# Spectral filter and token-shift MLP, two layers each: all queues in a written order, zero frequency left out, norm scale put into the first table

## The chip, the cores and the metric

The kernel runs on one core of a Trainium2 chip. The time is the device time in microseconds. The engines named here are TensorE (PE, with its weight loads as PEld), VectorE (DVE), ScalarE (ACT), GpSimd (POOL) and SyncE (SP, which here only issues DMAs). Each engine works through its own queue in order. Matmul results go to PSUM, which is used as eight banks of 128 x 512 float32.

## The reference

A row state x of 2048 x 512 goes through two pairs of layers: a spectral filter (A) and a token-shift MLP (B). Both take a normalized x and add their result to x.

```
def _A_ref(x, w_r, w_i):
    X = rfft2(x.astype(float32), axes=(-2, -1))
    X = X * (w_r + 1j * w_i)                      # w: 2048 x 257
    return irfft2(X, s=(S, D)).astype(bfloat16)

def _B_ref(x, w1, w2, w3, w4):
    h = gelu(layernorm(x) @ w1)                   # 512 -> 512
    # four column quarters of h, shifted by +1, -1, +2, -2 rows
    x1 = x + concatenate([g0, g1, g2, g3]) @ w2   # 512 -> 512
    return x1 + gelu(layernorm(x1) @ w3) @ w4     # 512 -> 1792 -> 512

x = x + A(layernorm(x)); x = x + B(layernorm(x))
x = x + A(layernorm(x)); x = x + B(layernorm(x))
```

## The kernel before

The 2048 rows are split as p x q: 128 on partitions, 16 tiles q of 128 x 512. The state x stays in SBUF as bfloat16 (`x_state`). The transform over the 2048 rows is done in two factors, 128 and 16; the transform over the 512 columns is one matrix with 256 real and 256 imaginary columns.

`load_all` issues the DMAs (x, the tables, the filter weights W, the MLP weights). `first_stats` computes the sums of the first norm. `fix_weights` prepares the two purely real frequencies, column 0 and column 256, which share a place: it reads W on POOL (`cw`, L263 and L264), mirrors it by a small matmul (`ps_cw`, L266 and L268) and writes a corrected first column and a factor `beta`.

`layer_A` has four loops one after the other. For each q, DVE subtracts the mean and scales (`xn`, L224), PE multiplies by the 128-point table T (`ps_V`, L295) and the result is copied to V. For each of 16 blocks b, PE transforms the columns (`ps_TV`, L310), ACT copies (`TV`, L313), PE makes the 16-point step (`ps_X`, L315 to L317), ACT copies (`X`), and after every second block DVE multiplies by W (`Pa`, `Pb`, `Z`). After every fourth block a mirrored column 0 is added (`ps_mir`, then five POOL steps). Then, for each b, PE does the inverse 16-point step (`ps_M`, L352 and L353), copied to M. Then, for each q, PE does the inverse over columns (`ps_Y`, L370), ACT copies (`Y`, L373), PE does the inverse 128-point step (`ps_y`, L375) and DVE adds to x with a sum (L376); ACT computes the sum of squares (L196), and per group of four q's POOL computes the norm (`finish`, ten small steps).

`layer_B` works on four groups of four q's: `w1(g)` normalizes (L224), transposes on PE (`pt`, L388) with a copy on ACT (`xT`, L391), multiplies (`ps_h`, L416) and applies GELU on ACT (`hT`, L418); ACT also writes the normalized row `xb` (L411). `w2(g)` multiplies the shifted rows (`ps_x`, L432), DVE adds `xb` (L433), the norm and transposes follow. `w3` (`ps_g`, L451) and `w4` (`ps_o`, L462) are 224 matmuls each a layer.

The program is written loop after loop, and a scheduler of the framework puts the instructions of each engine in order; the pools (eight PSUM banks in one ring, `stream` with four buffers) set what may be in flight. The diff touches almost the whole program.

## Time and profile before

| | before |
|---|---|
| time, median of 3 runs (lowest to highest) | 607.88 us (604.0 to 610.07) |
| profiled execution: time, span | 607.9 us, 606.1 us |
| PE busy | 419.0 us (69%), 2022 matmuls |
| ACT busy | 282.1 us (47%) |
| DVE busy | 172.4 us (28%) |
| POOL busy | 85.4 us (14%) |
| mean granted TensorE clock | 0.900 |

The profile is one execution. Busy matmul time counts the pipelined duration of each matmul, so the spacing of matmuls in a dense stretch tells more than the mean duration. A row of the groups gives the line, the engine, output and inputs by name, the shapes, the count, then busy time, mean ns of one, and the idle time of that engine before these instructions with what ended it. A row of the waits reads "engine, what it would run, what it waited for: total us, times, longest".

### The profile page before, as it was taken

Reading aid. Unit: us, or ns where it says so; the run is one execution under the profiler, and the core shown is the slowest. Engines: PE = TensorE matmul, PEld = TensorE weight load, DVE = VectorE, ACT = ScalarE, POOL = GpSimd, SP = SyncE. Lnnn points to the kernel's source line nnn. Section 1 sums busy time; section 2 is a strip of 40 time slices with the busy share of each in tenths; the row PEclk is TensorE's granted clock in tenths of the full one; section 3 lists DMA queues with packets and bytes.
Section 4 is the critical chain, followed back from the end, with each engine's and each line's share of the span. In section 5 each row is a group of like instructions: output and inputs, shape, how many; then the busy total and the mean of one; then the engine's idle time right before and its main releaser. Section 6 shows DMA issues by size and latency. Waiting matters only on the chain.

```text
span 606.1 us, 5633 instructions
## 1 busy us (share of the span) xinstructions
PE 419.0 (69%) x2022; PEld 202.2 (33%) x2060; DVE 172.4 (28%) x441; ACT 282.1 (47%) x530; POOL 85.4 (14%) x248
## 2 busy tenths in 40 slices
PE   0046675544666697999996667365567566999997
PEld 0033243112233343444443325111224333444443
DVE  5253453222044321111026446312122333010111
ACT  6124554556655565353424545455654555614310
POOL 5410110232111101011011010222200111000000
PEclk9999999676888797999998999957976889899999
DMA  9993000000000000000000000000000000010001
GB/s 299 106 335 136 1 1 0 0 0 2 0 1 1 0 1 0 1 1 1 0 1 1 1 1 1 1 0 0 1 0 1 1 1 1 0 36 10 26 27 43
DMA packets 12267, 15.70 MB, mean 26 GB/s; under 512 B 1104, under 2 KB 10192, under 8 KB 11984
## 3 DMA queue, kind: packets, MB, share of 16 engines
q1 hardware_dynamic: 11952, 14.79, 9.8%
q10 hardware_dynamic: 288, 0.56, 0.2%
q8 instruction: 16, 0.26, 0.2%
q14 instruction: 11, 0.09, 0.0%
HBM read 13.25 MB, written 2.10 MB: 25 GB/s over the span
## 4 chain that ended last, share of the span: by engine, by line
PE 57%; ACT 16%; DVE 9%; POOL 7%; issue 5%; DMA 5%; SPq 0%; POOLq 0%; ACTq 0%; DVEq 0%
PE ps_g L451 17%; PE ps_o L462 16%; PE ps_TV L310 5%; PE ps_h L416 5%; ACT junk L196 3%; POOL ln_r L216 3%; DVE xb L433 3%; ACT TV L313 3%; ACT xT L391 3%; DMA W<-in_A_w_i_dram 3%; PE ps_Y L370 3%; ACT Y L373 2%; PE ps_y L375 2%; PE pt L388 2%; ACT xb L411 2%
## 5 line engine op out<-in xcount | busy, mean ns | idle before, releaser
L451 PE MATMUL ps_g<-xT,w 128*128 128x512 bf16 x436 | 103.8, 394 | 1.0 <-issue 0.4
L462 PE MATMUL ps_o<-w,gT 128*128 128x512 bf16 x440 | 97.2, 379 | 0.4
L453 ACT ACTIVATE gT<-ps_g 128x512 bf16<-128x512 f32 x112 | 66.6, 597 | 54.9 <-PE ps_g L451 41.9
L196 ACT ACTIVATE junk<-x_state 128x512 bf16<-128x512 bf16 x64 | 40.0, 625 | 65.6 <-DVE x_state L468 37.2
L451 PEld LDWEIGHTS <-w 128*128 128x128 bf16 x448 | 45.4, 102 | 55.2 <-issue 6.7
L462 PEld LDWEIGHTS <-gT 128*128 128x128 bf16 x448 | 43.9, 98 | 52.8
L388 PE MATMUL pt<-ident,xn 128*128 128x128 bf16 x256 | 26.7, 286 | 37.1 <-DVE xn L224 37.1
L208 POOL TENSOR_SCALAR ln_m<-ln_s 128x4 f32<-128x4 f32 x24 | 7.3, 303 | 307.2 <-DVE xb L433 131.4
L375 PE MATMUL ps_y<-Y,Tinv 128*128 128x512 bf16 x32 | 15.4, 480 | 50.5 <-ACT Y L373 50.5
L416 PE MATMUL ps_h<-xT,w 128*128 128x512 bf16 x122 | 36.1, 452 | 20.1 <-ACT xT L391 19.6
L433 DVE SCALAR_TENSOR_TENSOR xb<-ps_x,xb 128x512 bf16<-128x512 f32 x32 | 21.6, 687 | 98.5 <-PE ps_x L432 98.3
L391 ACT ACTIVATE xT<-pt 128x1024 bf16<-128x1024 bf16 x32 | 31.2, 1027 | 34.2 <-PE pt L388 34.2
L370 PE MATMUL ps_Y<-G,M 128*128 128x512 bf16 x124 | 43.7, 479 | 2.2 <-DVE M L357 0.9
L376 DVE SCALAR_TENSOR_TENSOR x_state<-ps_y,x_state 128x512 bf16<-128x512 f32 x32 | 22.1, 691 | 73.1 <-PE ps_y L375 73.1
L370 PEld LDWEIGHTS <-M 128*128 128x128 bf16 x128 | 14.5, 114 | 79.6 <-issue 71.5
L388 PEld LDWEIGHTS <-xn 128*128 128x128 bf16 x256 | 23.5, 132 | 45.8 <-DVE xn L224 41.1
L310 PE MATMUL ps_TV<-FA,V 128*128 128x512 bf16 x122 | 35.6, 404 | 2.4 <-DVE V L301 1.8
L411 ACT ACTIVATE xb<-x_state,ln_nmr,ln_r 128x512 bf16<-128x512 bf16 x32 | 24.4, 804 | 26.0 <-POOL ln_nmr L220 26.0
L465 DVE TENSOR_TENSOR x_state<-ps_o,x_state 128x512 bf16<-128x512 f32 x16 | 11.1, 692 | 76.8 <-PE ps_o L462 76.8
L468 DVE SCALAR_TENSOR_TENSOR x_state<-ps_o,x_state 128x512 bf16<-128x512 f32 x16 | 11.1, 691 | 72.2 <-PE ps_o L462 72.2
L216 POOL TENSOR_TENSOR ln_r<-ln_ve,mhalf 128x4 f32<-128x4 f32 (+1 forms) x24 | 30.3, 1261 | 2.0
L318 ACT ACTIVATE X<-ps_X 128x512 bf16<-128x512 f32 x32 | 19.1, 597 | 22.9 <-PE ps_X L317 22.9
(84 smaller groups left out, 468.4 us busy)
## 6 DMA issues: line engine op xcount, KB each, us to landing
w<-in_B_w_dram SPq DMA_DIRECT2D x2, 1792.0 KB, 15.2
x_state<-in_A_x_dram SPq DMA_DIRECT2D x8, 256.0 KB, 5.4
out_dram<-x_state SPq DMA_DIRECT2D x16, 128.0 KB, 1.8
TL<-tab_TL SPq DMA_DIRECT2D x1, 1536.0 KB, 8.5
TR<-tab_TR SPq DMA_DIRECT2D x1, 1536.0 KB, 10.7
w<-in_B_w_dram SPq DMA_DIRECT2D x2, 512.0 KB, 10.7
W<-in_A_w_r_dram SPq DMA_DIRECT2D x7, 128.5 KB, 9.6
W<-in_A_w_i_dram SPq DMA_DIRECT2D x7, 128.5 KB, 8.7
```

Of the source, the lines that this page charges most:

```text
L196: K.nc.scalar.activation(junk[:], src, ACT.Square, bias=0.0, scale=1.0, accum_out=self.ss[:, i:i + 1])
L216: e.tensor_tensor(self.r[:, 0:n], ve[:, 0:n], K.mhalf[:, 0:n], op=ALU.pow)
L310: nc.tensor.matmul(ps[:], lhsT=V[:, t, b].rearrange("d q c -> d (q c)"), rhs=K.FA[:, t, :], start=(t == 0), stop=(t == 3))
L370: nc.tensor.matmul(ps[:], lhsT=M[:, F, e, q, :], rhs=K.G[:, F, e, :], start=(n == 0), stop=(n == 3))
L388: nc.tensor.transpose(pt[:, (i % 2) * 4 + t, :], src[:, t * P:(t + 1) * P], K.ident[:])
L391: nc.scalar.activation(xT[:, :, o:o + 2 * P].rearrange("p t (h c) -> p t h c", h=2), pt[:].rearrange("p (h t) c -> p t h c", h=2), ACT.Cop ...
L411: nc.scalar.activation(xb[:, q, :], K.x[:, q, :], ACT.Identity, bias=L.nmr[:, i:i + 1], scale=L.r[:, i:i + 1])
L416: nc.tensor.matmul(ps[:], lhsT=K.w1[:, t, j * P:(j + 1) * P], rhs=xT[:, t, :], start=(t == 0), stop=(t == 3))
L433: nc.vector.scalar_tensor_tensor(xb[:, q, :], ps[:], 1.0, xb[:, q, :], op0=ALU.mult, op1=ALU.add, accum_out=L.s[:, i:i + 1])
L451: nc.tensor.matmul(ps[:], lhsT=K.w3[:, c, t * P:(t + 1) * P], rhs=xT[:, c, :], start=(c == 0), stop=(c == 3))
L453: nc.scalar.activation(gT[:, t, :], ps[:], ACT.Gelu_apprx_tanh, bias=0.0, scale=1.0)
L462: nc.tensor.matmul(ps[:], lhsT=gT[:, t, i * P:(i + 1) * P], rhs=K.w4[:, t, :], start=(t == 0), stop=(t == 13))
```

## The change

The framework's scheduler is switched off: each engine's queue is the order in which the program is written, and the program is written anew for that.

- *Zero frequency.* A normalized row has mean zero, so frequency 0 of the columns is zero. The table now holds frequencies 1 to 256, and frequency 256 alone takes the last imaginary column (its cosine column is zero). `fix_weights`, `Pm`, `beta` and the mirrored column are gone. Blocks of the 128-point factor are numbered anew (j = 16 jj + b), and W is loaded in 24 transfers instead of 16.
- *Norm scale in the first table.* For A, the mean is not subtracted (it only moves frequency 0), and the scale multiplies T per row: DVE makes `Tq` = T r (128 x 128), and PE uses x itself as the stationary operand (`front`).
- *Statistics.* DVE `bn_stats` and `bn_aggr` replace the sums on DVE and squares on ACT, except before w3 (sum with the add, squares on ACT) and for five of the first 16 tiles (both sums on ACT). The small steps run on DVE, the power on POOL.
- *xb.* The once normalized row, which `xb` held, is made inside w2's add from the twice normalized `xn` and a factor `c` per row.
- *Order.* `middle` takes the column transform of block i, the 16-point step of block i-1 and the inverse step of block i-5 in one step, 21 steps. `mlp` begins with 24 steps in which the return of tile s (`back_d`), of tile s-1 (`back_p`), the norm, transposes, w1 and the first half of w2 are mixed; the other half of w2 is mixed into the first group of w3. The next layer's fronts follow the groups of w4.

ScalarE's queue in the return from the frequency domain, ahead of the change. `Y` is the copy of `ps_Y`, `junk` a sum of squares, `xb` the once normalized row:

```order
L373 ACTIVATE Y<-ps_Y 128x512
L196 ACTIVATE junk,ln_ss<-x_state 128x512
L373 ACTIVATE Y<-ps_Y 128x512
L411 ACTIVATE xb<-x_state,ln_nmr,ln_r 128x512 x2
L196 ACTIVATE junk,ln_ss<-x_state 128x512
L373 ACTIVATE Y<-ps_Y 128x512
```

The same place now. `xT` are transposed rows, `hT` is GELU of w1:

```order
L132 ACTIVATE Y<-ps_Y 128x512 x8
L132 ACTIVATE xT<-pt 128x4x256 x2
L132 ACTIVATE Y<-ps_Y 128x512
L408 ACT_TABLE_LOAD
L408 ACTIVATE hT<-ps_h 128x4x128
L132 ACTIVATE Y<-ps_Y 128x512
L408 ACTIVATE hT<-ps_h 128x4x128
```

The squares and `xb` no longer stand between the copies, and the work of the MLP's first product stands among them.

TensorE's queue at the same stage, before; the numbers tell the tiles apart, and `Y_803` is the copy of `ps_Y_798`:

```order
L370 LDWEIGHTS M_270
L370 MATMUL ps_Y_798<-G_111,M_270 128x512
L375 LDWEIGHTS Tinv_113
L375 MATMUL ps_y_805<-Y_803,Tinv_113 128x512
L370 LDWEIGHTS M_270
L370 MATMUL ps_Y_810<-G_111,M_270 128x512
```

And now, where `Y_731` is the copy of `ps_Y_726`, the product ahead of `ps_Y_740`:

```order
L366 LDWEIGHTS M_374
L366 MATMUL ps_Y_740<-G_117,M_374 128x512
L373 LDWEIGHTS Tinv_119
L373 MATMUL ps_y_747<-Y_731,Tinv_119 128x512
L366 LDWEIGHTS M_374
L366 MATMUL ps_Y_753<-G_117,M_374 128x512
```

The product that reads the copy of one tile now stands behind the next tile's `ps_Y` instead of right behind its own.

VectorE's queue at the end of the frequency stage, before:

```order
L324 TENSOR_TENSOR Pa<-X,W 128x1024
L324 TENSOR_TENSOR Pb<-X,W 128x1024
L338 COPY mir<-ps_mir 128x8
L326 TENSOR_TENSOR Z<-Pa,Pb 128x2x256
L327 TENSOR_TENSOR Z<-Pa,Pb 128x2x256
L357 CAST M<-ps_M 128x64x8 x8
L376 SCALAR_TENSOR_TENSOR x_state,ln_s<-ps_y,x_state 128x512 x4
```

And now:

```order
L320 TENSOR_TENSOR Z<-Pab 128x2x256
L331 CAST M<-ps_M 128x64x8
L317 TENSOR_TENSOR Pab<-X,W 128x1024 x2
L319 TENSOR_TENSOR Z<-Pab 128x2x256
L320 TENSOR_TENSOR Z<-Pab 128x2x256
L331 CAST M<-ps_M 128x64x8 x3
L374 TENSOR_TENSOR x_state<-ps_y,x_state 128x512
L191 BN_STATS ln_st<-x_state 128x6
```

The casts to M, which stood in one run behind all products with W, now alternate with them, with three left at the end.

The diff, cut to what the rest speaks of:

```diff
-            j = 4 * b + jj
+            j = 16 * jj + b
...
-    f = np.arange(256)
+    f = np.arange(1, 257)
...
+    cos[:, 255] = 0.0
...
-    ln = first_stats(K)
-    fix_weights(K)
-    ln = layer_A(K, ln)
-    ln = layer_B(K, ln, last=False)
-    ln = layer_A(K, ln)
-    layer_B(K, ln, last=True)
+    ctx.enter_context(tc.manual_schedule())
...
+    first_front(K)
+    for last in (False, True):
+        middle(K)
+        mlp(K, last)
...
+def front(K, q, r, eng):
+    nc = K.nc
+    Tq = K.stream.tile([P, P], BF16, name="Tq")
+    nc.vector.tensor_scalar(Tq[:], K.T[:], r, None, op0=ALU.mult)
+    ps = bank(K, "ps_V")
+    for t in range(4):
+        nc.tensor.matmul(ps[:, t * P:(t + 1) * P], lhsT=K.x[:, q, t * P:(t + 1) * P], rhs=Tq[:], start=True, stop=True)
...
+def first_front(K):
...
+    for g in range(5):
+        if g < 4:
+            L = Stats(K)
...
+            L.rstd()
+        if prev:
+            for i in range(4):
+                front(K, 4 * g - 4 + i, prev.r[:, i:i + 1], "VS"[i % 2])
+        prev = L
...
+    LAG = 5
+    for i in range(NB + LAG):
+        if i < NB:
+            over_d(i)
+        if 1 <= i <= NB:
+            over_q(i - 1)
+        if i >= LAG:
+            back_q(i - LAG)
...
+    def back_p(q):
+        g, i = divmod(q, 4)
+        ps = bank(K, "ps_y")
+        nc.tensor.matmul(ps[:], lhsT=K.Tinv[:], rhs=Ys.pop(q)[:], start=True, stop=True)
+        nc.vector.tensor_tensor(K.x[:, q, :], ps[:], K.x[:, q, :], op=ALU.add)
+        if i == 0:
+            ln[g] = Stats(K)
+        ln[g].bn(i, K.x[:, q, :])
+        if i == 3:
+            ln[g].rstd_twice()
...
+    for s in range(24):
+        if s < NQ:
+            back_d(s)
+        if 1 <= s <= NQ:
+            back_p(s - 1)
+        g, r = divmod(s - 5, 4)
+        if r == 0 and 0 <= g < 4:
+            norm2(g)
+        g, r = divmod(s - 7, 4)
+        if r == 0 and 0 <= g < 4:
+            tr(g, 0)
+            tr(g, 1)
+        g, r = divmod(s - 8, 4)
+        if 0 <= g < 4:
+            w1(g, r)
+        if s == 20:
+            norm3(0)
+        if s == 21:
+            apply3(0)
+        if s == 23:
+            tr3(0, 0)
+            tr3(0, 1)
+        g, r = divmod(s - 16, 4)
+        if 0 <= g < 2:
+            w2(g, r)
+    for t in range(14):
+        w3(0, t)
...
+        if t % 2 == 0 and t < 8:
+            w2(2, t // 2)
...
+    for i in range(4):
+        w4(3, i)
+        if not last and i < 2:
             for c in range(4):
...
+                fr(i, c, "S")
+    if not last:
+        for c in range(4):
+            fr(2, c, "S")
+        for c in range(4):
+            fr(3, c, "SVSV"[c])
```

## The prediction

> **What bounds the kernel now.** I read the page's totals and its forty slices first, then the busy time by stretch, then who waited for whom, and last single rows for durations.

> ```profile
> span 606.1 us, 5633 instructions
> PE 419.0 (69%) x2022; PEld 202.2 (33%) x2060; DVE 172.4 (28%) x441; ACT 282.1 (47%) x530; POOL 85.4 (14%) x248
> PE   0046675544666697999996667365567566999997
> ```

> TensorE (PE) is the busiest engine and the slices show two humps at 9, with valleys of 4 to 7 between them: no engine is the bound in the valleys, so a chain of waits is. By stretch (columns: length, then busy us and count for PE, PEld, DVE, ACT, POOL, then TensorE's granted clock, DMA share, GB/s; the last two stretches were asked for PE alone):

> ```profile
> 48.00:86.50 38.50, 24.97 (x112) 11.13 (x114) 14.50 (x31) 18.83 (x32) 3.82 (x15) 1.00 0.08 29
> 95.00:152.00 57.00, 28.75 (x99) 10.71 (x101) 13.77 (x40) 30.12 (x62) 13.49 (x38) 0.75 0.00 0
> 152.00:210.00 58.00, 36.22 (x202) 19.95 (x205) 18.59 (x56) 32.35 (x57) 8.54 (x24) 0.85 0.00 0
> 260.00:319.00 59.00, 58.74 (x271) 1.00 0.00 1
> 87.00:94.50 7.50, 7.08 (x65) 1.00 0.01 2
> ```

> In 260 to 319 us (w3 and w4) PE is busy 58.74 of 59.00 us: 271 matmuls, 0.218 us each, at full clock. In 95 to 152 us it does 99 in 57 us, at a granted clock of 0.75. The waits say why:

> ```profile
> PE ps_cw L266 <- POOL cw L264: 35.7, 1, 35.7
> PE ps_y L375 <- ACT Y L373: 50.5, 32, 4.8
> PE pt L388 <- DVE xn L224: 37.1, 8, 4.9
> PE ps_X L315 <- ACT TV L313: 23.4, 32, 0.7
> PE ps_h L416 <- ACT xT L391: 19.6, 8, 5.1
> ```

> (total us, times, longest.) They sum to 166 us. In each, PE has issued a product, waits for ACT or DVE to copy it, and has nothing else next in its queue; the first waits for the filter weights to arrive before any other PE work. The stage boundaries come from four rows:

> ```profile
> 47.21 0.59 PE L310 MATMUL ps_TV<-FA,V 128*128 128x512 bf16 x1 [0.88 <-DVE V L301]
> 94.91 1.02 PE L370 MATMUL ps_Y<-G,M 128*128 128x512 bf16 x3 [0.83 <-ACT M L359]
> 233.05 3.18 PE L451 MATMUL ps_g<-xT,w 128*128 128x512 bf16 x7
> 319.14 0.69 DVE L468 SCALAR_TENSOR_TENSOR x_state<-ps_o,x_state 128x512 bf16<-128x512 f32 x1 [2.32 <-PE ps_o L462]
> 328.65 0.58 PE L310 MATMUL ps_TV<-FA,V 128*128 128x512 bf16 x1 [0.89 <-DVE V L301]
> 602.58 0.69 DVE L465 TENSOR_TENSOR x_state<-ps_o,x_state 128x512 bf16<-128x512 f32 x1 [2.33 <-PE ps_o L462]
> ```

> So the first layer now spends 47.2 us before its first row transform, 47.7 in the frequency stage, 138.1 from the return to the first dense w3, 86.1 dense, 9.5 to the next layer.

> **The change, stage by stage.** The matmuls of each kind stay, so I price each stage by its PE work, then ask what ends later. Prices: 0.218 us for 512 columns (above), 0.115 for 256 (7.50/65), and for 128 columns, taking the last one's 0.26 us off the row below, (1.37-0.26)/15 = 0.075; I use 0.08.

> ```profile
> 326.39 1.37 PE L295 MATMUL ps_V<-T,xn 128*128 128x128 bf16 x16 [1.12 <-DVE xn L224]
> L224 DVE TENSOR_SCALAR xn<-x_state,ln_m,ln_r 128x512 bf16<-128x512 bf16 x64 | 23.0, 408 | 13.5 <-POOL ln_r L216 13.2 <-PE ps_V L295 0.3
> L465 DVE TENSOR_TENSOR x_state<-ps_o,x_state 128x512 bf16<-128x512 f32 x16 | 11.1, 692 | 76.8 <-PE ps_o L462 76.8
> L324 DVE TENSOR_TENSOR Pa<-X,W 128x1024 bf16<-128x1024 bf16 x16 | 11.1, 692 | 50.7 <-ACT X L318 50.7
> L326 DVE TENSOR_TENSOR Z<-Pa,Pb 128x512 bf16<-128x512 bf16 x16 | 6.8, 425 | 0.3
> L440 DVE TENSOR_TENSOR x_state<-x_state,xb 128x512 bf16<-128x512 bf16 x32 | 12.8, 419 | 0.1
> L301 DVE CAST V<-ps_V 128x512 bf16<-128x512 f32 x16 | 10.6, 685 | 1.3 <-PE ps_V L295 1.3
> L338 DVE COPY mir<-ps_mir 128x8 f32<-128x8 f32 x8 | 1.3, 158 | 0.0
> L313 ACT ACTIVATE TV<-ps_TV 128x512 bf16<-128x512 f32 x32 | 19.1, 597 | 19.8 <-PE ps_TV L310 19.8
> L391 ACT ACTIVATE xT<-pt 128x1024 bf16<-128x1024 bf16 x32 | 31.2, 1027 | 34.2 <-PE pt L388 34.2
> 322.18 1.04 POOL L216 TENSOR_TENSOR ln_r<-ln_ve,mhalf 128x4 f32<-128x4 f32 x1
> ```

> bn_stats and bn_aggr have no row. bn_stats reads 512 elements: from below the 0.41 us of the xn row, from above two passes of the x_state row, 1.38. I take 0.69, the row of that size that also gives one result per element. bn_aggr I take as the 0.16 us COPY. [...]

> *Start.* The weight wait of 35.7 us leaves the head of the PE queue; the first reader of W is now the DVE product, behind all 16 front steps. These rows set the new start:

> ```profile
> 4.16 0.69 DVE L236 SCALAR_TENSOR_TENSOR junk<-x_state 128x512 bf16<-128x512 bf16 x1 [4.16 <-DMA x_state<-in_A_x_dram]
> 17.76 0.31 SPq L159 DMA_DIRECT2D W<-in_A_w_i_dram  x1
> 20.25 0.31 SPq L159 DMA_DIRECT2D W<-in_A_w_i_dram  x1
> 35.20 0.23 POOL L263 COPY cw<-W 128x32 bf16<-128x32 bf16 x1 [12.26 <-DMA W<-in_A_w_i_dram]
> ```

> DVE is the long queue: 4.2 us to the first x, 11 x (0.69+0.16) = 9.4 statistics, 16 scaled tables at 0.2 (between 0.16 and 0.41) = 3.2, 8 casts = 5.5, and before each cast about 0.7 us for two tiles' eight matmuls on PE = 5.6. That is 28; small self-waits of DVE and the first norm (POOL) bring my estimate to 33. W: 24 transfers instead of 16, with the same rows. Between the two SP rows a transfer, a 15-row piece and a 1-row piece went in 2.49 us, twice 1.24, so the eight extra small pieces cost nothing if rows pace the queue, and 8 x 0.7 = 5.6 us if pieces do. At 35.2 W is there before the first product is due (PE's first back step comes five steps after 33, at about 39), so I take no cost; at 41, with the tables queued behind W on SP, it costs 4 to 6.

> *Frequency stage.* Per layer 80 x 0.218 + 96 x 0.115 = 28.5 us of PE. ACT carries 40 x 0.60 = 24, DVE 8 x (2 x 0.69 + 2 x 0.42 + 0.69) = 23, both now beside PE. The mirror (5 POOL steps, a small matmul and a copy for every fourth block) goes; it lay partly in those valleys and earns nothing more. At the end the last product (0.6 + 2.2 on DVE) stands before the last back step and cast: 3 us bare. 31.5, against 47.7.

> *Return and first half of the MLP* (24 written steps). PE: 64 matmuls of back_d, 16 of back_p, 64 of w1 and 32 of w2 are 176 x 0.218 = 38.4, and 80 transposes 6.4: 44.8. Up to step 7 DVE is longer: add 0.69, statistics 0.85 and about 0.1 of waits on itself, 1.65 a step against PE's 1.09; the first transposes need five steps of it, the norm and 4 x 0.41, 12.7 us, where PE arrives at 8.7. 4 us of wait, 1 more for xT (1.03 twice on ACT): 50. The xb copies of ACT disappear (their product is now made on DVE in w2's add), and the POOL chain of ten steps becomes two powers of 1.04 us. The norm's own wait for the first of them is new on DVE, with the next tile's add queued behind it; between the two the order puts three small steps, an add and statistics, 1.9 us, so the wait is covered. Without them it would cost 1 us a group, 4 a layer.

> *First w3 group with the rest of w2.* 88 x 0.218 + 32 x 0.08 = 21.7, 1 of wait: 23. Here DVE's normalized copy waits for the POOL power with the next w2 add behind it; that add's bank is asked for again three steps later, over 2.6 us on, so 1.04 is hidden. The 16 residual adds (0.42 each) move in here and into the next group, where DVE has room. So 73 us stand for the 138.1.

> *Dense rest.* w3(1) with 16 transposes 13.5, then 336 x 0.218 = 73.2: 86.7, as before. ACT's 0.60 a tile stays under PE's 0.87.

> *Seam.* The mean is no longer subtracted and the norm multiplies a 128-column table in place of the 512-column row (0.41 before, 0.2 now), on DVE beside PE. Two front groups (2.6) lie in w4's last rows; behind its last matmul stand add 0.69, statistics 0.85, a small step 0.16, power 1.04, table 0.2, four matmuls 0.5, cast 0.69 and some 0.5 of handovers: 4.6. Together 7.2.

> Sum: 33 + 2 x (31.5 + 50 + 23 + 86.7) + 7.2 + 3.5 (the last add, then the output, 602.58 to 606.1) = 426.1 span. The profiled execution took 607.9 for a span of 606.1, 1.8 around it (and 607.88 is the median, of runs from 604.0 to 610.07, so it stands for them): 428. For waits I can't place I add one of 0.73 (23.4/32, the TV row above) in every tenth of the 118 interleaved steps (21, 24 and 14 a layer), 8.6: **437 us**.

> **The rivals.** *DVE becomes the bound of the return stage.* If bn_stats takes 1.38 us, a step of the first 16 costs 2.3 on DVE; 16 of these, the norms and 2.3 of lead give 48, and 14 us of PE follow: 62 for 50. Twice that, and 11 x 0.69 in the start: 437 + 24 + 7.6 = 469. For it: no row prices the instruction. Against: no 512-element DVE row is over 0.7.

> *The clock stays low.* At 0.75, as in 95 to 152 us, the 95 us of PE work of the interleaved stages become 127 per layer: 437 + 64 = 501. [...]

> *One step of lag is not enough (slower).* If each written step still ends in a bare wait of PE on ACT or DVE, the price is the mean of the ps_y row, 50.5/32 = 1.58, plus the 0.16 small DVE step now queued before each release: 118 x 1.74 + 428 = 633. It ends slower, by over 1%, once the mean wait passes (614 - 428)/118 = 1.58 us. Against: with one step between, PE has 0.87 us or more to hide ACT's 0.60, and eight PSUM banks turn over about every 2.7 steps.

> *It doesn't do what it says*, for example since W still holds everything or banks serialize the steps: 600 to 610. The queue order itself is visible and different, so this needs something unseen.

> **How the numbers follow.** Forecast, 418 to 455: 0.63. DVE price, up to 478: 0.17. Clock: 0.11. Slower: 0.03. No effect: 0.02. Under 418: 0.04 (all waits vanish and the start falls to 28). The range 418 to 478 holds the first two and so 0.8; W at 41 us lies inside. About 1% is what the runs can tell from no change, so faster 0.95, same 0.02, slower 0.03.

> **What would show it.** Right: no PE row waiting on a weight copy, and the first ps_TV near 33 us; 30 to 33 us between the first ps_TV and the first ps_Y; about 73 from there to the solid w3; PE at 9 in nearly all slices after the second, clock 0.95 or more; waits of ps_y on Y and ps_X on TV near zero; a wait of the transposes on DVE of 3 to 5 us once a layer. Wrong: bn_stats over 0.8 us, DVE above 80% in the return stage, clock below 0.9 there, or a PE wait repeated at each step.

## The result, and the profile after

The changed kernel takes 437.02 us (median of 4 runs, 434.69 to 438.38) against 607.35 us (median of 4, 604.0 to 610.07) of the kernel before in the same session: a ratio of 0.719, 95% interval 0.7145 to 0.7241. The profiled execution took 437.16 us for a span of 435.4. A few executions below were slow as a whole (901 us for 522 in one case), so times, ratios and intervals go by the fast ones: all four where no other number is given.

The page of the changed kernel, its totals, TensorE's forty slices and the granted clock:

```profile
span 435.4 us, 5373 instructions
PE 379.7 (87%) x2048; PEld 189.9 (44%) x2048; DVE 215.1 (49%) x547; ACT 214.3 (49%) x396; POOL 39.3 (9%) x65
PE   0237997799799999999966998979889999999996
PEclk9999999899999999999997799889999999999999
```

Most of the valleys of 4 to 7 are filled; what is left of them is the start (2, 3, 7), four slices of 7 in and around the returns, two slices of 6 in the middle, the passage to the second layer, and the tail. DVE did more than before (215.1 for 172.4 us), ACT and POOL less. Who waited for whom on TensorE (total us, times, longest):

```profile
PE ps_V L241 <- DVE Tq L238: 34.6, 15, 11.7
PE pt L393 <- DVE xn L230: 4.7, 2, 2.3
PE ps_g L452 <- ACT xT L132: 3.1, 2, 1.6
PE ps_h L406 <- ACT xT L132: 2.7, 4, 0.9
```

The waits of `ps_y` on Y (50.5 us), of `ps_X` on TV (23.4) and of `ps_cw` on the weights (35.7) are not in the list any more; those of `pt` on xn and of `ps_h` on xT fell from 37.1 to 4.7 and from 19.6 to 2.7. One wait is new and large: the fronts (`ps_V`) wait 34.6 us for their scaled tables, of which the first 11.7 is the arrival of x and the first norm. The rows at the stage boundaries, in the order of time:

```profile
36.81 3.60 PE L294 MATMUL ps_TV<-FA,V 128*128 128x512 bf16 x8 [0.69 <-ACT V L132]
69.24 1.89 PE L366 MATMUL ps_Y<-G,M 128*128 128x512 bf16 x8 [0.90 <-ACT M L132]
119.59 1.02 PE L452 MATMUL ps_g<-xT,w 128*128 128x512 bf16 x4 [1.54 <-ACT xT L132]
239.33 3.57 PE L294 MATMUL ps_TV<-FA,V 128*128 128x512 bf16 x8 [0.88 <-DVE V L244]
273.20 3.28 PE L366 MATMUL ps_Y<-G,M 128*128 128x512 bf16 x8 [0.95 <-DVE M L331]
324.89 1.02 PE L452 MATMUL ps_g<-xT,w 128*128 128x512 bf16 x4 [1.60 <-ACT xT L132]
431.37 0.69 DVE L462 TENSOR_TENSOR x_state<-ps_o,x_state 128x512 bf16<-128x512 f32 x1 [2.33 <-PE ps_o L460]
```

The windows of the first layer (length, then busy us and count for PE, PEld, DVE, ACT, POOL, the clock, DMA share, GB/s; of the last for PE alone):

```profile
36.80:69.20 32.40, 30.12 (x176) 17.57 (x176) 21.33 (x40) 21.57 (x40) 0.00 (x0) 1.00 0.40 140
69.20:119.60 50.40, 45.10 (x257) 22.09 (x258) 39.01 (x105) 33.80 (x58) 9.10 (x9) 0.97 0.00 1
119.60:141.20 21.60, 21.60 (x124) 1.00 0.00 1
```

The clock of 1.00 in the first row can't be right for its first 3.4 us: the eight `ps_TV` at 36.81 take 3.60 us, those of the run with the scheduler on 1.90 (shown below).

Set against the prediction, in us of the span:

| stage | before | predicted | measured |
|---|---|---|---|
| start, to the first `ps_TV` | 47.2 | 33 | 36.8 |
| frequency stage, layers 1 and 2 | 47.7, 48.2 | 31.5 | 32.4, 33.9 |
| first `ps_Y` to first w3, layers 1 and 2 | 114.0, 115.8 | 50 | 50.4, 51.7 |
| first w3 to the end of w4, layer 1 (with two front groups) | 110.2 | 112.3 | 112.7 |
| the same, layer 2 | 109.9 | 109.7 | 106.5 |
| seam behind the last w4 product | 9.5 | 4.6 | 7.0 |
| tail | 3.5 | 3.5 | 4.0 |
| waits I couldn't place | | 8.6 | see below |

Before, the w2 of groups 0 to 2 lay ahead of the first w3, now only those of groups 0 and 1, so the third and fourth rows don't hold quite the same work. From the return to the second group's w3, with all of w2 and the first group's w3, it took 138.1 us; now it takes 71 to 72 (50.4 and the 21.6 of the last window, which reaches a few matmuls into the next group).

### The profile page after: what moved, and what is told of

Same layout as the page of the kernel before. It is cut to its first block, busy times and chain, and to the rows that moved or that the text cites. A ratio compares the mean times of both kernels' runs of the same rounds, so it can differ in the third digit from the quotient of the medians.

```text
span 435.4 us, 5373 instructions
## 1 busy us (share of the span) xinstructions
PE 379.7 (87%) x2048; PEld 189.9 (44%) x2048; DVE 215.1 (49%) x547; ACT 214.3 (49%) x396; POOL 39.3 (9%) x65
## 3 DMA queue, kind: packets, MB, share of 16 engines
q1 hardware_dynamic: 11904, 14.72, 13.2%
## 4 chain that ended last, share of the span: by engine, by line
PE 75%; DVE 9%; DMA 8%; ACT 6%; issue 1%; POOL 0%; ACTq 0%; SPq 0%; DVEq 0%; POOLq 0%
PE ps_g L452 22%; PE ps_o L460 22%; PE ps_TV L294 7%; PE ps_Y L366 5%; PE ps_x L420 4%; PE ps_h L406 4%; DMA W<-in_A_w_r_dram 4%; ACT xT L132 3%; PE pt L393 2%; DVE ln_st L191 2%; DMA TR<-tab_TR 2%; PE ps_X L304 1%; DMA W<-in_A_w_i_dram 1%; DVE x_state L374 1%; PE ps_V L241 1%; ACT junk L425 1%
## 5 line engine op out<-in xcount | busy, mean ns | idle before, releaser
L462 DVE TENSOR_TENSOR x_state<-ps_o,x_state 128x512 bf16<-128x512 f32 x32 | 22.1, 692 | 125.6 <-PE ps_o L460 125.6
L241 PE MATMUL ps_V<-Tq,x_state 128*128 128x128 bf16 x128 | 13.9, 276 | 34.6 <-DVE Tq L238 34.6
L191 DVE BATCH_NORM_STATS2 ln_st<-x_state 128x6 f32<-128x512 bf16 x59 | 40.8, 691 | 6.1 <-DMA x_state<-in_A_x_dram 4.4
L294 PE MATMUL ps_TV<-FA,V 128*128 128x512 bf16 x128 | 36.8, 418 | 1.6 <-DVE V L244 0.9
L406 PE MATMUL ps_h<-xT,w 128*128 128x512 bf16 x128 | 33.9, 389 | 2.7 <-ACT xT L132 2.7
L422 DVE SCALAR_TENSOR_TENSOR xn<-xn,ln_c,ps_x 128x512 bf16<-128x512 bf16 x32 | 23.5, 745 | 20.6 <-PE ps_x L420 20.5
L317 DVE TENSOR_TENSOR Pab<-X,W 128x1024 bf16<-128x1024 bf16 x32 | 20.8, 689 | 24.4 <-ACT X L132 24.2
L420 PE MATMUL ps_x<-w,hT 128*128 128x512 bf16 x128 | 32.8, 379 | 0.0
L212 POOL TENSOR_TENSOR ln_r<-ln_ve,mhalf 128x4 f32<-128x4 f32 (+1 forms) x19 | 17.5, 923 | 154.9 <-DVE ln_ve L211 154.9
L425 ACT ACTIVATE junk<-xn 128x512 bf16<-128x512 bf16 x32 | 20.1, 629 | 21.8 <-DVE xn L422 21.7
L132 ACT ACTIVATE TV<-ps_TV 128x512 bf16<-128x512 f32 x32 | 19.1, 597 | 17.9 <-PE ps_TV L294 16.9
L132 ACT ACTIVATE Y<-ps_Y 128x512 bf16<-128x512 f32 x32 | 19.1, 598 | 16.4 <-PE ps_Y L366 16.4
L374 DVE TENSOR_TENSOR x_state<-ps_y,x_state 128x512 bf16<-128x512 f32 x32 | 21.5, 672 | 7.3 <-PE ps_y L373 7.3
```

Of the source, the lines that this page charges most:

```text
L132: K.nc.scalar.activation(dst, src, ACT.Copy, bias=0.0, scale=1.0)
L191: v.bn_stats(st[:], src)
L241: nc.tensor.matmul(ps[:, t * P:(t + 1) * P], lhsT=K.x[:, q, t * P:(t + 1) * P], rhs=Tq[:], start=True, stop=True)
L294: nc.tensor.matmul(ps[:], lhsT=V[:, t, b].rearrange("d q c -> d (q c)"), rhs=K.FA[:, t, :], start=(t == 0), stop=(t == 3))
L374: nc.vector.tensor_tensor(K.x[:, q, :], ps[:], K.x[:, q, :], op=ALU.add)
L406: nc.tensor.matmul(ps[:], lhsT=K.w1[:, t, j * P:(j + 1) * P], rhs=xT[g][:, t, :], start=(t == 0), stop=(t == 3))
```

## The experiments

Times are medians, with the kernel before run beside them (607.2, 604.0 and 605.0 us in the three sessions). Between sessions I compare the ratios to it.

**The order apart from the operations.** The new operations in the old order, with the scheduler on:

```diff
-    ctx.enter_context(tc.manual_schedule())
...
-    LAG = 5
-    for i in range(NB + LAG):
...
+    for i in range(NB):
+        over_d(i)
+        over_q(i)
+    for i in range(NB):
+        back_q(i)
...
+    for q in range(NQ):
+        back_d(q)
+        back_p(q)
+    w1g(0)
+    w1g(1)
+    w2g(0)
...
```

> Same result as the changed kernel. The new operations (statistics, scale in the first table, no zero frequency, xb made in w2's add) in the order of the kernel before: stage behind stage, each product right ahead of the product that reads its copy, the framework's scheduler on. Theory, the order carries most of the gain: the waits of PE on ACT's copies (ps_X on TV 23.4 us, ps_y on Y 50.5 us in the trace of before) stay, the first in size and the second shortened because the squares are gone from ACT; the wait on the filter weights (35.7) and the POOL steps of the norms go. I work out 37 start + 2 x (43 frequency, 38 return, 65 first half of the MLP, 86 dense) + 10 seam + 5 = 516, between 490 and 560. Rival, the operations carry it: under 465. Rival, the operations alone earn nothing beyond the weight wait: 590 to 600.

It took 521.8 us (three runs), ratio 0.860 (0.857 to 0.863). The operations alone are thus worth 85 us, and the order, with the scheduler switched off, the other half (0.860 to 0.719 of the time before, some 85 us). With the scheduler on in both, by the next run, the order is worth 0.860 to 0.699. Theory and number agree; neither rival does. Where this kernel's time goes is not shown by a profile here, so the expected stages aren't tested.

**The scheduler on, the written order kept.** One line is taken out:

```diff
-    ctx.enter_context(tc.manual_schedule())
```

> Same result. The changed kernel with only the line that switches the framework's scheduler off taken out. Theory, what matters is the order in which the program is written, not who puts it into the queues: 437, within 1%. Rival, the scheduler moves small steps of DVE, ACT or POOL ahead of those that others wait for: 445 to 470, with the difference in one engine's waits.

It took 424.15 us, ratio 0.699 (0.695 to 0.703), against 0.719 (0.7145 to 0.7241) for the changed kernel. My theory falls, and the rival too, on the other side: switching the scheduler off costs 12 to 13 us. TensorE's queue is almost the same in both; DVE's is not. The start in the changed kernel, DVE and then PE:

```profile
12.34 0.69 DVE L244 CAST V<-ps_V 128x512 bf16<-128x512 f32 x1 [0.68 <-PE ps_V L241]
12.95 0.41 DVE L238 TENSOR_SCALAR Tq<-T,ln_r 128x128 bf16<-128x128 bf16 x2
20.07 0.17 DVE L211 TENSOR_SCALAR ln_ve<-ln_mv 128x4 f32<-128x4 f32 x1 [3.30 <-POOL ln_mv L272]
...
13.25 1.01 PE L241 MATMUL ps_V<-Tq,x_state 128*128 128x128 bf16 x8 [0.94 <-DVE Tq L238]
```

The same with the scheduler on:

```profile
12.53 0.74 DVE L237 TENSOR_SCALAR Tq<-T,ln_r 128x128 bf16<-128x128 bf16 x4 [0.42 <-POOL ln_r L211]
...
15.67 1.87 PE L240 MATMUL ps_V<-Tq,x_state 128*128 128x128 bf16 x16 [0.96 <-DMA W<-in_A_w_r_dram]
23.09 1.90 PE L293 MATMUL ps_TV<-FA,V 128*128 128x512 bf16 x8 [0.69 <-ACT V L131]
```

In the written order each cast to V stands on DVE ahead of the next two tables. The cast waits for PE, the tables wait behind the cast, and PE waits 0.94 us for the tables; between groups, ACT's copies stand ahead of its sums for the next norm, and DVE waits 3.30 us for them. The scheduler puts four tables together and the statistics early: the first `ps_TV` stands at 23.1 instead of 36.8. The passage to the second layer is shorter too (4.3 us behind the last w4 product, for 7.0), while its returns are longer (52.9 and 53.1, for 50.4 and 51.7). (The DMA that the second PE row names is no input of these products.)

**The lag taken away.**

```diff
-        if 1 <= i <= NB:
-            over_q(i - 1)
+        if i < NB:
+            over_q(i)
...
-        if 1 <= s <= NQ:
-            back_p(s - 1)
+        if s < NQ:
+            back_p(s)
```

> Same result. The changed kernel, but the 16-point step of block i stands right behind the column transform of block i, and the last step of the return of tile s right behind the first of tile s: lag 0 instead of 1, all else as it is. Theory, the one step of lag is what hides ACT's copy: 32 waits of ps_X on TV and 32 of ps_y on Y of 0.73 us come back, part of the latter hidden behind DVE in the first seven steps of the return: 437 + 23 + 18 = 478, between 462 and 500 (the higher end if the gaps also lower the clock). Rival, the other interleaved work (inverse steps, w1, w2) and the eight banks hide the copy anyway: 437 to 445.

481.6 us (three runs), ratio 0.794 (0.791 to 0.797). Its waits on PE:

```profile
PE ps_y L373 <- ACT Y L132: 23.5, 30, 1.2
PE ps_X L302 <- ACT TV L132: 22.7, 32, 0.7
```

62 waits, 46.2 us, for a loss of 45 us (0.794 less 0.719): each copy of 0.60 us with its handovers shows fully as soon as nothing stands between, although inverse steps, w1 and eight banks were there to help. The frequency stage takes 45.6 and 43.9 us, the return 61.1 and 61.2. So one step of lag hides all of it, and the lag is about half of what the order is worth (45 of some 85 us).

**The statistics twice as dear.**

```diff
+        st2 = self.K.small.tile([P, 6], FP32, name="ln_st2")
+        v.bn_stats(st2[:], src)
         v.bn_stats(st[:], src)
```

> Same result, with each of the 59 statistics made twice on DVE (the first copy is not used): 0.69 us more each, as if the instruction took 1.38. By the prediction's rival on the price of the statistics: +24 in the two return stages and +7.6 in the start, 469, and PE's transposes and adds wait on DVE there. Rival, DVE's spare time (49% busy in the changed kernel) takes it: 437 to 443.

456.7 us, ratio 0.753 (0.750 to 0.756): 20 us slower, between the two. The return, and PE's wait for DVE there:

```profile
71.60:131.80 60.20, 48.69 (x257) 23.04 (x258) 48.37 (x121) 33.90 (x58) 9.09 (x9) 0.91 0.00 1
PE pt L395 <- DVE xn L232: 15.3, 6, 5.3
```

DVE is now busy 48.4 of 60.2 us there (39.0 of 50.4 in the changed kernel), and PE waits for its transposes 15.3 us instead of 4.7: the return takes 9.8 us more in the first layer and 8.5 in the second. The start grew by only 2.5 (first `ps_TV` at 39.3), though 11 statistics more are 7.6 us: DVE had been waiting there for PE, ACT and POOL.

**The start rewritten, the seam rewritten, both.** In the start, statistics stand as early as their data, and four tables ahead of the casts of the group before. In the seam, the tables of a front group stand ahead of the add of the w4 tile behind which PE wants them:

```diff
+    act_stats(2)
+    for q in (0, 1, 3, 4, 6):
+        dve_stats(q)
+    Ls[0].rstd()
...
+    ts = tables(0)
+    Ls[1].rstd()
...
+    fronts(0, ts)
+    ts = tables(1)
...
     for i in range(4):
+        ts = [tq(min(i, 3), c) for c in range(4 if i < 3 else 3)]
         w4(3, i)
-        if not last and i < 2:
+        if i < 3:
             for c in range(4):
-                fr(i, c, "S")
+                mm(i, c, ts[c], "S")
...
+    ts.append(tq(3, 3))
+    for c in range(4):
+        mm(3, c, ts[c], "S")
```

> Same result. The changed kernel with only the first fronts rewritten: all statistics as early as their data, ACT's sums ahead of ACT's copies, and the four scaled tables of a group ahead of the casts of the group before. Theory, the written order of the start costs the time: in the changed kernel each cast to V stands on DVE ahead of the next scaled table, and PE waits 0.95 us after every second tile and 3 to 5 us for the sums of groups 2 and 3. First ps_TV from 36.8 to about 24 (DVE alone: 4.1 + 11 x 0.85 + 16 x 0.17 + 8 x 0.65 = 21.4 and some waits); about 3 come back in waits on W and TR, whose transfers don't get earlier: 427, between 423 and 430. Rival, the transfers bound the start: 433 to 437.

423.5 us (two runs), ratio 0.701 (0.6965 to 0.705): the theory's lower end, and not the rival.

> Same result. The changed kernel with only the passage to the second layer rewritten: the scaled tables of a group of fronts stand on DVE ahead of the add of the w4 tile behind which PE uses them, the last group's first three ahead of the last add, and the third group's products stand between the last two w4 tiles. Theory, the three waits of PE of 2.1 us in w4's last rows, 2.5 of the 7.0 us seam and the slow stretch of TensorE behind it go: 437 - 4 - 2.5 - 2 = 428, between 426 and 432. Rival, the chain behind the last add (add, statistics, power, table, product, copy) sets the seam whatever stands before it: 433 to 437.

428.6 us, ratio 0.710 (0.706 to 0.713). PE in w4's last rows and the seam, in the changed kernel:

```profile
219.04 1.05 PE L241 MATMUL ps_V<-Tq,x_state 128*128 128x128 bf16 x16 [2.08 <-DVE Tq L238]
...
234.38 2.12 PE L241 MATMUL ps_V<-Tq,x_state 128*128 128x128 bf16 x24 [2.08 <-DVE Tq L238]
237.44 1.01 PE L241 MATMUL ps_V<-Tq,x_state 128*128 128x128 bf16 x8 [0.94 <-DVE Tq L238]
```

And with the seam rewritten:

```profile
219.26 1.06 PE L244 MATMUL ps_V<-Tq,x_state 128*128 128x128 bf16 x16
...
234.06 0.40 PE L244 MATMUL ps_V<-Tq,x_state 128*128 128x128 bf16 x4 [2.22 <-DVE Tq L236]
235.15 1.90 PE L301 MATMUL ps_TV<-FA,V 128*128 128x512 bf16 x7 [0.69 <-ACT V L132]
```

Four waits became one, which is the chain of the last tile; the `ps_TV` behind it take 1.90 us for seven instead of 3.57 for eight. The seam is 3.9 us, and the second frequency stage 30.7 instead of 33.9.

> Same result. Both rewritings together. If they act in different places of the span: 437 - 10 - 8.5 = 418.5, between 414 and 422, so some 2 to 6 below the same program with the framework's scheduler. Rival, they don't add up: 424 or more.

416.65 us, ratio 0.689 (0.687 to 0.692). The two add up: of the time before, 0.018 and 0.010 alone, 0.030 together. It is also faster than the scheduler's order. The first `ps_TV` and, in this kernel as in the one with the scheduler on, a wait on the transfers:

```profile
22.84 0.61 PE L327 MATMUL ps_TV<-FA,V 128*128 128x512 bf16 x1 [0.69 <-ACT V L132]
...
PE ps_M L359 <- DMA TR<-tab_TR: 3.3, 1, 3.3
```

**Loads in halves, and the return shifted by one step.**

```diff
-    table("TL", nc.sync)
+    half("TL", 0)
...
-    for k in ("TR", "G", "Tinv"):
+    half("TR", 0)
+    half("TL", 1)
+    half("TR", 1)
+    for k in ("G", "Tinv"):
...
-    for s in range(24):
+    for s in range(25):
...
-        g, r = divmod(s - 7, 4)
+        g, r = divmod(s - 8, 4)
```

> Same result. Both rewritings, and two more: the tables TL and TR are loaded in halves (TL's first half ahead of W, TR's first half right behind W), and transposes, w1, and what follows stand one step later in the return. Theory: the waits on W and TR (3) go, and of the 2.35 us wait of the transposes about 1.1 a layer, with the slow stretch of TensorE behind it (1.5 a layer): 418.5 - 3 - 5 = 410.5, between 407 and 414. Rival, the ring of eight banks holds PE back at the same point, because the adds on DVE are late whatever stands next on PE: 414 to 418.

415.1 us, ratio 0.687 (0.683 to 0.691): the rival's number. The first frequency stage fell from 36.2 to 33.2 us, the 3 us of the loads. The shift earned nothing in sum (return 51.7 and 50.4, against 50.4 and 50.3; 1.4 of the 51.7 are a slow stretch of TensorE, eight `ps_Y` in 3.26 us for 1.89 in the second layer). The rival is half right: DVE is late, but no wait of PE on a bank shows. The transposes did come closer to their data; the wait went elsewhere. PE, ACT and DVE in the return:

```profile
68.26 1.37 PE L435 MATMUL pt<-ident,xn 128*128 128x128 bf16 x16 [1.27 <-DVE xn L239]
98.12 1.02 PE L448 MATMUL ps_h<-xT,w 128*128 128x512 bf16 x4 [2.89 <-ACT xT L132]
...
93.33 0.63 ACT L467 ACTIVATE junk<-xn 128x512 bf16<-128x512 bf16 x1 [4.41 <-DVE xn L464]
...
92.55 0.74 DVE L464 SCALAR_TENSOR_TENSOR xn<-xn,ln_c,ps_x 128x512 bf16<-128x512 bf16 x1
```

DVE reaches the first w2 add at 92.55. ACT's square of that row waits 4.41 us for it, with GELUs and the copies xT queued behind, and PE then waits 2.89 us for xT where the changed kernel waited under 1 (0.9 at most).

**The loads without the shift; the shift with later squares.**

> Same result. The rewritten start and passage with the tables in halves, without the shift of the return by one step. In the run with all four, 3 us of the frequency stage were won by the loads, and the shift won nothing in the return: the transposes' wait fell from 2.35 to 1.27, but a wait of w1 on the copies xT rose to 2.9. Theory: 416.65 - 3 = 413.6, level with or below the run of all four (415.1). Rival, the shift did earn its part and the loads did not: 416 or more.

414.2 us, ratio 0.685 (0.683 to 0.688). So the loads carry their part (the interval just overlaps that of the two rewritings alone, 0.687 to 0.692) and the shift none; from the run of all four it can't be told apart by time. The last edit keeps the shift and puts each square behind the next GELU:

```diff
+    late = []
+    def squares():
+        while late:
+            g, i = late.pop(0)
...
     def w2(g, i):
...
+        squares()
+        late.append((g, i))
```

> Same result. All four rewritings, and the squares of each w2 tile stand one step later in ScalarE's queue, behind the next GELU. Theory, in the run of all four ScalarE's first square waits 4.4 us for a late add on DVE, with the GELU of w1 and the copies xT queued behind it, and this gave the shift's gain back: the wait of w1 on xT of 2.9 a layer falls below 1, the second half of the return gets 2 to 3 us a layer shorter: 415 - 5 = 410, between 408 and 412.5. Rival, DVE itself is late there (adds, statistics and norms without a gap up to the first w2 add), so that the wait only moves to another product: 413 to 416.

412.4 us, ratio 0.682 (0.679 to 0.685), the fastest of all, though its interval overlaps that of the two runs before it. Its return is 49.4 us in both layers, and the wait that was 2.89 is

```profile
94.52 1.02 PE L448 MATMUL ps_h<-xT,w 128*128 128x512 bf16 x4 [1.79 <-ACT xT L132]
90.83 0.63 ACT L459 ACTIVATE junk<-xn 128x512 bf16<-128x512 bf16 x1 [2.67 <-DVE xn L473]
```

so the square still stands in the way, less long. Of the expected 5 us some 2 came: the return is 1.0 us shorter in each layer than in the run of all four, once the slow stretch of 1.4 is taken off there. Part of the wait was thus the square's place; that the rest is DVE being late, as the rival says, is argued from the row and not tested.

**The scheduler on the rewritten program.**

```diff
-    ctx.enter_context(tc.manual_schedule())
```

> Same result. The program with rewritten start, passage and loads, with the framework's scheduler on. The changed kernel was 13 us slower than the same program with the scheduler, and the rewriting has taken that from the start and the passage. Theory, the scheduler has nothing left to mend and its own order of the return costs it what it did before (52.9 against 50.4 us a layer): 413.6 + 2 to 5 = 417. Rival, it finds a better order in the return of this program too: under 412.

421.4 us (three runs), ratio 0.695 (0.692 to 0.699), 7 us slower than the same program in its written order. So the written order earns between 1 and 2% where it is written well, and costs 3% where it isn't. Between the two profiled spans lie 6.4 us: 1.1 in each frequency stage, 2.4 in the second return, 1.7 from the first w3 to the end of w4 in the first layer, 0.1 elsewhere. That the scheduler's return is slower in both layers, as expected, is not borne out (51.7 for 51.9 in the first).

**The weight wait alone.** In the kernel before, the preparation of the two real frequencies was moved behind the first fronts:

```diff
-    fix_weights(K)
...
+    if not hasattr(K, "beta"):
+        fix_weights(K)
     for b in range(NB):
         if b % 4 == 0:
```

> Same result. The kernel before, with the preparation of the two real frequencies moved behind the first fronts, so that PE's 64 ps_V products no longer stand behind the 35.7 us wait for W. Theory, this wait alone costs what lies between W's arrival and the first ps_TV: PE makes the fronts before W is there, and the first ps_TV goes from 47.2 to about 37: 604 to 607 less 10, 595. Rival, the later POOL steps (beta) or the first Z wait instead, and nothing is earned: over 602.

593.4 us against 605.0, ratio 0.982 (0.977 to 0.987). PE, at the place that was blocked for 35.7 us:

```profile
32.16 0.16 PE L265 MATMUL ps_cw<-cw,Pm 128*128 128x4 bf16 x1 [3.95 <-POOL cw L263]
32.26 1.86 PE L311 MATMUL ps_TV<-FA,V 128*128 128x512 bf16 x4
```

The first `ps_TV` stood at 47.2 and now stands at 32.3. A wait of 35.7 us at the head of PE's queue cost 11.6 (8 to 14 by the interval): what counts is the work that stood behind it and could have been done meanwhile. That the first `ps_TV` came 15 us earlier and the time fell by less is not explained here. The 11.6 are about a seventh of the 85 us that the operations brought; which of the other operations brought the rest is not shown by a run.

## Why the prediction was right, step by step

*Which waits bound the kernel, and that the change removes them.* Right. Of the five waits named there (166 us) three are gone from the list of the changed kernel and two are down to 4.7 and 2.7 us; without the lag 46.2 us of them return.

*Frequency stage, 31.5.* 32.4 and 33.9, but not quite by the sum as written. The 3 us bare at the end measured 2.25 (waits of 1.35 and 0.90). What the sum put at nothing is slow stretches of TensorE: both layers begin with eight `ps_TV` in 3.60 and 3.57 us, where the same eight take 1.90 in the run with the scheduler on, and in the second the slow stretch goes on to 245.3, 6 us after the stage's start.

*Return and first half of the MLP, 50.* 50.4 and 51.7. The transposes' wait on DVE, predicted at 4, is 2.35 (PE arrives 8.6 us into the stage, as forecast, and DVE's chain takes 10.9 and not 12.7), with some 2 us lost in the slow matmuls behind it, and the waits on xT come to 2.9 (0.50, 0.87 and, at the end, 1.54), for 1 forecast; 16 transposes take 0.89 us (89.97 to 90.86), not the 1.28 of my price of 0.08 each. The row that I took the price from stood behind a wait of 1.12, and the first row below, behind one of 2.35, shows the same 1.37. So the stage came out right with terms too high and too low that nearly cancel:

```profile
80.17 1.37 PE L393 MATMUL pt<-ident,xn 128*128 128x128 bf16 x16 [2.35 <-DVE xn L230]
81.37 1.79 PE L366 MATMUL ps_Y<-G,M 128*128 128x512 bf16 x4
89.97 1.06 PE L393 MATMUL pt<-ident,xn 128*128 128x128 bf16 x16
90.86 1.03 PE L406 MATMUL ps_h<-xT,w 128*128 128x512 bf16 x4
```

That price is also part of why the second layer's dense part is 3.2 below its term (106.5 for 109.7): 48 transposes make 1.2 of it, and the wait of 1 us that I put into the first w3 group doesn't stand in it (21.60 of 21.60 us busy in the window above) but just ahead of it, 1.54 and 1.60, where it counts to the return.

*The price of the statistics.* Right by the row it was taken from:

```profile
L191 DVE BATCH_NORM_STATS2 ln_st<-x_state 128x6 f32<-128x512 bf16 x59 | 40.8, 691 | 6.1 <-DMA x_state<-in_A_x_dram 4.4
```

0.691 us for the 0.69 forecast. The rival's own price, had it come true, was set too high: doubled statistics cost 20 us, not 32; 5.1 of the error lie in the start (2.5 for 7.6) and 5.7 in the two returns (18.3 for 24).

*Start, 33.* Mis-sized: 36.8. The sum counted DVE's own work and PE's time per pair of tiles, and called the rest "small self-waits of DVE and the first norm". The rest was DVE waiting for ACT's sums through POOL, 6.2 us in three places: 1.6 for the first norm, and 4.6 where ACT's sums stand behind ACT's copies. PE's time per pair cost 1.3 more than the 5.6 forecast (0.68 to 0.97 us each), since TensorE was slow in the start: 8 products of 128 columns in 1.01 us, where 16 take 1.05 later. That W would cost nothing was right: its first reader, which DVE starts at 42.98, was waiting for ACT. A row of DVE's waits and that reader:

```profile
DVE ln_ve L211 <- POOL ln_mv L272: 6.2, 3, 3.3
...
42.98 1.49 DVE L317 TENSOR_TENSOR Pab<-X,W 128x1024 bf16<-128x1024 bf16 x2 [7.52 <-ACT X L132]
```

*Seam, 7.2.* Mis-sized: the two front groups inside w4's last rows were priced by their products alone (2.6), but each had a wait of 2.08 in front, because its tables stand behind an add that waits for PE; behind the last product 7.0 us for 4.6, as casts stand ahead of the last tables. With the 1.8 that the products took, together 13.0 for 7.2.

*The 8.6 of waits "in every tenth of the 118 interleaved steps".* The size was needed, the place was wrong. The measured stages stand 9.3 us above my sum without it (435.4 for 426.1): 3.8 in the start, 3.3 in the frequency stages, 2.1 in the returns, 0.4 in the first dense part (two waits of 2.08 against the cheaper rest), 2.4 in the seam, 0.5 in the tail, less 3.2 in the second dense part. No wait repeats at every tenth step, and in the frequency stages and returns the slow stretches of TensorE account for the excess and more. That the allowance came out right is luck: it hid two faults of the order that could have been read from it before any run, and whose repair is worth 18 to 20 us.

*The clock at 0.75.* It didn't come: by the column 0.97 to 1.00 in the windows above, and 0.90 and 0.94 in the second layer's frequency stage and return. But the full clock that the forecast took for granted didn't come either: in these four stages TensorE worked 19 us slowly (3.4, 3.4, 6.0, 2.9 and 3.4), an estimate of 9.5 us lost, half of it, by the rates of the products. *One step of lag.* Enough, as argued. *Slower.* Nothing pointed there in any run. *The signs.* Some were set too sharp: PE is at 9 in 26 of 40 slices and not in nearly all, and the transposes wait 2.35 us and not 3 to 5.

## To other kernels

When an order is written out by hand, go through each engine's queue and ask of every instruction that waits for another engine what stands behind it that doesn't need it: here a cast ahead of a small table and a copy ahead of a sum cost 11 us together (0.018 of the time before), an add ahead of a table 6 (0.010), a square ahead of a copy some 2, and a scheduler had got the start and the passage right. One written step between a product and the reader of its copy was enough here to hide a 0.6 us copy, and without it such copies showed in full (62 waits, 46.2 us). Price a wait by the work that stands behind it and could have run, not by its length: here 35.7 us of wait cost 11.6.

## What the runs showed of the hardware

TensorE went slow after gaps of 1.35 and 0.90 us, and not each time. Two kernels with the same two gaps, at the end of the frequency stage: first the one without the shift, then the fastest one:

```profile
54.43 0.28 PE L368 MATMUL ps_M<-TR,Z 128*128 128x256 bf16 x1 [1.35 <-DVE Z L361]
56.60 3.41 PE L408 MATMUL ps_Y<-G,M 128*128 128x512 bf16 x8 [0.90 <-ACT M L132]
```

```profile
52.66 0.28 PE L368 MATMUL ps_M<-TR,Z 128*128 128x256 bf16 x1 [1.36 <-DVE Z L361]
54.84 1.89 PE L408 MATMUL ps_Y<-G,M 128*128 128x512 bf16 x8 [0.90 <-ACT M L132]
```

Eight products take 3.41 us in one and 1.89 in the other. So the length of the gaps alone doesn't decide it. What goes with it can be read from the traces, when the clock column is asked in short stretches. In the changed kernel it is 0.50 from 81.49 to 84.90 us, 235.09 to 245.33, 272.64 to 276.05 and 286.29 to 289.70: lengths and distances are whole multiples of 3.41 us. Cut on this grid, the two places above read (columns as before), first the one without the shift:

```profile
52.90:56.31 3.41, 1.40 (x10) 0.70 (x8) 3.38 (x7) 0.97 (x2) 0.00 (x0) 1.00 0.00 0
56.31:59.72 3.41, 3.12 (x8) 1.20 (x9) 0.19 (x1) 0.60 (x1) 0.00 (x0) 0.50 0.00 0
```

```profile
49.72:53.13 3.41, 2.00 (x17) 1.29 (x15) 3.29 (x8) 1.70 (x4) 0.00 (x0) 1.00 0.00 0
53.13:56.55 3.42, 2.52 (x15) 1.29 (x14) 1.61 (x3) 1.19 (x2) 0.00 (x0) 1.00 0.00 0
```
